# Attention's lead-in and first cycle: how bias rows are made, where the tails are turned, in which order bias rows and tails are asked for

## The chip, the core and the metric

The kernel runs on one core of one Trainium2 chip. A core has five engines that run beside one another, each through its own list of instructions in order: TensorE (PE in the profile, with PEld for its weight loads), VectorE (DVE), ScalarE (ACT), GpSimd (POOL) and SyncE (SP), which here issues nearly all transfers. An instruction that needs another engine's result, or a transfer's, waits at the head of its list, and all behind it waits too. The metric is the device time of one execution in microseconds (us).

## The reference

Three stages; the change lies in the first. q, k and v are 2 batches x 8 heads x 576 rows x 64.

```
scores = q k^T / 8
cum    = cumsum(max(s, 0))                       # per head, over the 576 rows
bias   = -(cum[i] - cum[j])
scores = where(j > i, -1e9, scores + min(bias, 0))
attn   = softmax(scores)
x      = attn v                                  # 1152 rows x 512
x      = (h cos h) w_out, with h = x w_in        # first expert layer, 512 x 2048 and back
out    = routed experts(x)                       # top 1 of 8, w1 512 x 1024, w2 1024 x 512
```

## The kernel before, in words

**Pairs and tails.** Heads are worked two at a time: 8 pairs, numbered 0 to 7, four of each batch. Of a head's 576 rows, 512 are four full tiles of 128; the last 64, the *tail*, are kept apart, for all four pairs of a batch together (tiles `qt`, `kt`, `vt`, and `wt` for their halves). A number in float32 is carried as two float16 halves (hi and lo), and q and k are turned so that the 64 columns of a head lie along the partitions; a matmul of `qT` and `kT` then has two parts, c = 0 with hi and lo, and c = 1 with hi and six more rows that carry the bias: `cum`, split into three float16 parts, for q, and the constants for k, and the other way round. These six are the *bias rows*.

**Lead-in.** `cums` (L190) sums s by a scan, turns the sums into PSUM, copies them to `cc` and writes the three parts to `bias_`, for q and k at once. `a_first` prepares pair 0 and the tails of the first batch on the engines: hi halves by ScalarE, lo halves by GpSimd, turns by TensorE (`turn_`: four turns into one PSUM bank, and one copy out of it). For all later pairs the turned halves come by a transposing transfer (`q_T`), and the bias rows by way of DRAM: `bias_` is turned to `bT` by a transfer, stored as `bt`, and read back into `qT` and `kT` (`pair_bias`, by SyncE).

**Cycles.** Then attention runs in cycles. The table `CYCLE` holds one cycle's work as pairs of a name and an offset: in cycle i the entry (name, o) runs `o_name` for pair i - o, if there is one. `tc.keep_in_program_order` keeps each engine's list in the order in which the table emits it. So the table sets the order of all engines and of SyncE's transfers. The names that matter here: S scores (the first S of a cycle starts it on TensorE), SD and S4 scores of the tail, M the mask and minimum, E the exponential, T the turn of probabilities and C its copy, NB spreading the row sums into `rsb` on GpSimd, R turning them on TensorE, KH and KL the halves of a later pair on GpSimd, LQK the loads of q and k, BK the bias rows of k, TR q's turning transfer and its bias rows, DUP the doubling of `kT` and `qT` on GpSimd, W a weight load for the next stage. Three entries serve the second batch's tails: LT loads them (`qt`, `kt`, four transfers; pair 4 stands for the batch), KTL splits them on GpSimd, TT turns them by transfers. LT has offset -4, so it runs at the end of cycle 0; KTL has -2 and runs near the start of cycle 2, ahead of NB.

**PSUM.** Banks come in four kinds of two: `s`, `pt`, `mm`, `sm`. A new use of a kind waits until one of its two banks has been read out.

Of the kernel before, what the change touches and what calls it, by code (L numbers as in the profile page):

```python
# [36 lines left out]
PB = 3  # L37
# [38 lines left out]
def kernel(ctx, tc, q, k, v, s, w_in, w_out, wg, w1, w2, out, cap, wide):  # L76
# [115 lines left out]
    def cums(pool):  # L192
# [138 lines left out]
    def a_first(ap):  # L331
# [11 lines left out]
        def dup_(w_, f, x):
            V(nc.scalar.copy, w_[:, 1, :, 0, :], halves(w_[:, 0], x)[0])

        def turn_(w_, t, c, a, f, i):
            pt = bank(*BANKS[i % 3], F16)
            m = KB if c else 128
            for j in range(4):
                tr_(pt[0:m, j * 128:(j + 1) * 128], w_[:, c, a + j, :, :].rearrange("p b d -> p (b d)")[:, 0:m], idh)  # L350
            V(f, t[0:m, c, a:a + 4, :].rearrange("p a t -> p (a t)"), pt[0:m, 0:512])
# [8 lines left out]
        for z in tail_:  # L360
            lo_(*z)
        d["qT"], d["kT"] = room(ap, "q", 2 * FULL, PB), room(ap, "k", 2 * FULL, 2)
        tl["qT"], tl["kT"] = room(ap, "qt", NP, 2), room(ap, "kt", NP, 2)
        for w_, f, x in work_:
            o = x * BW
            V(nc.vector.tensor_copy, w_[:, 1, :, 1, 0:6], bias_[:, o:o + 12 * FULL].rearrange("p (k c) -> p k c", c=6))
        for w_, f, x in tail_:
            o = x * BW
            V(nc.vector.tensor_copy, w_[:, 1, :, 1, 0:6], bias_[:, o:o + NP * NB * 6].rearrange("p (a c) -> p a c", c=NB * 6)[:, :, 12 * FULL:12 * FULL + 6])
        i = 0  # L370
        for c in range(2):
            for w_, f, x in work_:
                for a in (0, 4):
                    turn_(w_, d["qk"[x] + "T"], c, a, nc.vector.tensor_copy if c else nc.scalar.copy, i)
                    i += 1
        for z in tail_:
            dup_(*z)
        for c in range(2):
            for w_, f, x in tail_:
# [1003 lines left out]
```

## Time and profile before

| what | us |
|---|---|
| median of 3 runs | 434.71 |
| lowest and highest | 433.16, 439.06 |
| the profiled execution | 437.53 |
| its span, first to last instruction | 435.8 |
| TensorE busy | 401.6 (92%) |
| VectorE, ScalarE, GpSimd busy | 312.6, 275.6, 150.0 |

Attention's cycles start, by their first S on TensorE, at 15.46, 23.14, 33.91, 43.72, 53.28, 63.53, 73.09 and 82.66 us; the first expert layer runs to about 196 us, and the routed experts fill the rest. In the profile a busy share is an average over stages with different limits, and matmuls are pipelined, so a busy TensorE is not TensorE at its peak. The granted clock (PEclk) tells at what share of 2.4 GHz TensorE ran; 0.50 is 1.2 GHz. A row of the timeline gives the start, the duration, the engine, the line and the tiles, written first, then `<-`, then read; SPq is SyncE's queue of transfers, and its duration is that of the issue, not of the transfer.

### The profile page before, as it was taken

To read this page: it belongs to the slowest core of one execution; us is meant where nothing else is said; L and a number is where in the kernel's file an instruction comes from. 1 tells how busy PE (TensorE), PEld (TensorE's weight loads), DVE (VectorE), ACT (ScalarE), POOL (GpSimd) and SP (SyncE) were. 2 spreads that over 40 slices of the span, in tenths; PEclk is the share of its full clock that TensorE was granted. 3 is DMA by queue.
4 is the path that set the end of the run, shared out by engine and by line. 5 is a ranking of instruction groups with operands and counts; after the bars stand their busy time and mean duration, and the time that the engine had idled before them with its cause. 6 is when DMAs were issued, how large, how long until landed. Compare 5 with 4: busy or idle time off the path is not lost.

```text
span 435.8 us, 10790 instructions
## 1 busy us (share of the span) xinstructions
PE 401.6 (92%) x4008; PEld 291.5 (67%) x4008; DVE 312.6 (72%) x767; ACT 275.6 (63%) x634; POOL 150.0 (34%) x242
## 2 busy tenths in 40 slices
PE   2799999999999999989999999797999999798893
PEld 1588888886666666544444454355988999798862
DVE  7769999749998499989875665654824576667570
ACT  6679989977888577775234433525536667677560
POOL 7668888553454345445000032010011012022030
PEclk9989999999999999999999999899999999899898
DMA  7979995103389933312567476758697689888741
GB/s 164 206 169 195 165 214 142 52 2 99 97 231 304 335 121 99 96 57 90 193 186 236 111 160 225 221 127 252 206 213 159 178 277 251 312 280 278 250 133 39
DMA packets 91228, 77.61 MB, mean 178 GB/s; under 512 B 64006, under 2 KB 72198, under 8 KB 91167
## 3 DMA queue, kind: packets, MB, share of 16 engines
q1 hardware_dynamic: 87855, 71.85, 60.2%
q0 software_dynamic: 2256, 4.73, 3.2%
q8 instruction: 33, 0.54, 0.6%
q10 hardware_dynamic: 1056, 0.26, 0.3%
q14 instruction: 28, 0.23, 0.2%
HBM read 57.66 MB, written 12.36 MB: 161 GB/s over the span
## 4 chain that ended last, share of the span: by engine, by line
PE 30%; DMA 11%; DVE 7%; ACT 5%; issue 5%; SPq 2%; POOL 1%; POOLq 0%; ACTq 0%; DVEq 0%
DMA ws<-in_moe_w_dram 9%; PE ps_mm L865 6%; PE ps_sm L865 4%; PE ps_mm L1064 3%; PE ps_s L1042 2%; PE ps_pt L865 2%; PE ps_s L865 2%; PE ps_pt L1042 2%; PE ps_pt L1064 2%; PE ps_mm L1042 2%; PE ps_s L1064 2%; DVE gall L657 2%; ACT gall L656 2%; DMA xr<-row 1%; DVE ws L679 1%
## 5 line engine op out<-in xcount | busy, mean ns | idle before, releaser
L810 PEld LDWEIGHTS <-win 128*128 128x128 f16 x576 | 56.2, 98 | 37.9 <-issue 1.1
L865 PEld LDWEIGHTS <-gall 128*128 128x128 f16 x432 | 41.3, 99 | 50.5 <-issue 4.0
L865 PE MATMUL ps_mm<-wout,gall 128*128 128x512 f16 x240 | 57.9, 387 | 1.3 <-DVE n__2934 L824 1.3
L1051 POOL DMA_INDIRECT out_dram<-gall,eM x16 | 20.2, 1266 | 101.8 <-ACT gall L1050 94.1
L657 DVE SCALAR_TENSOR_TENSOR gall<-ws,gall 128x1024 f16<-128x1024 f32 x32 | 38.7, 1220 | 23.0 <-ACT gall L656 22.6
L656 ACT ACTIVATE gall<-ws 128x1024 f16<-128x1024 f32 x32 | 33.6, 1058 | 26.9 <-DMA ws<-in_moe_w_dram 26.8
L656 ACT ACTIVATE wout<-ws 128x512 f16<-128x512 f32 (+1 forms) x32 | 27.2, 860 | 27.7 <-DVE ws L679 20.3
L239 ACT ACTIVATE z<-z,st 128x256 f32<-128x256 f32 (+4 forms) x72 | 41.9, 587 | 0.8 <-DVE st L239 0.8
L239 DVE CUSTOM_DVE_ANT_0 z<-ps_s,zm 128x512 f32<-128x512 f32 (+3 forms) x72 | 34.5, 510 | 10.2 <-PE ps_s L242 9.0
L945 POOL DMA_INDIRECT disp<-row,rsli x9 | 9.2, 1020 | 93.9 <-ACT rm L926 48.6
L657 DVE SCALAR_TENSOR_TENSOR wout<-ws,wout 128x512 f16<-128x512 f32 (+1 forms) x32 | 30.3, 954 | 10.7 <-ACT wout L656 10.6
L810 PE MATMUL ps_s<-xT,win 128*128 128x384 f16 x192 | 34.1, 326 | 0.0
L810 PE MATMUL ps_pt<-xT,win 128*128 128x384 f16 x192 | 33.8, 326 | 0.0
L810 PE MATMUL ps_mm<-xT,win 128*128 128x384 f16 x192 | 33.8, 326 | 0.0
L245 PE MATMUL ps_pt<-idf,z 128*128 128x128 f32 x192 | 30.2, 282 | 1.3 <-DVE p L239 1.3
L823 ACT ACTIVATE y<-y,quarter 128x384 f32<-128x384 f32 x48 | 29.2, 609 | 0.1
L239 ACT COPY p<-ps_pt 128x512 f32<-128x512 f32 (+2 forms) x48 | 25.2, 525 | 6.0 <-PE ps_pt L245 5.7
L657 DVE SCALAR_TENSOR_TENSOR win<-ws,win 128x1024 f16<-128x1024 f32 x16 | 19.5, 1224 | 12.4 <-ACT win L656 12.1
L1042 PEld LDWEIGHTS <-gall 128*128 128x128 f16 x480 | 27.9, 97 | 0.7 <-DVE gall L657 0.6
L245 PEld LDWEIGHTS ps_pt<-idf,z 128*128 128x128 f32 x192 | 23.1, 145 | 6.3 <-issue 1.5
L1064 PEld LDWEIGHTS <-gall 128*128 128x128 f16 x384 | 23.9, 101 | 2.8 <-issue 2.8
L242 PE MATMUL ps_s<-kT,qT 128*128 128x384 f16 (+7 forms) x128 | 24.1, 307 | 1.0 <-DMA kT<-bt 0.5
(497 smaller groups left out, 897.2 us busy)
## 6 DMA issues: line engine op xcount, KB each, us to landing
ws<-in_moe_w_dram SPq DMA_DIRECT2D x64, 512.0 KB, 5.3
ws<-in_moe_w_in_dram SPq DMA_DIRECT2D x16, 512.0 KB, 5.3
ws<-in_moe_w_out_dram SPq DMA_DIRECT2D x16, 512.0 KB, 4.0
disp<-zc SPq DMA_DIRECT2D x18, 257.0 KB, 7.2
out_dram<-zc SPq DMA_DIRECT2D x9, 256.0 KB, 4.7
qf<-in_q_dram SPq DMA_DIRECT2D x16, 128.0 KB
vf<-in_v_dram SPq DMA_DIRECT2D x16, 128.0 KB, 2.9
kf<-in_k_dram SPq DMA_DIRECT2D x14, 128.0 KB, 3.5
```

The lines of the kernel that those rows point to most:

```text
L239: return pin(f(*a, **kw))
L242: return pin(nc.tensor.matmul(out_, **kw))
L245: return pin(nc.tensor.transpose(out_, in_, id_))
L656: nc.scalar.activation(hi, src, AF.Copy, scale=sc)
L657: (eng or nc.vector).scalar_tensor_tensor(lo, src, sc, hi, ALU.mult, ALU.subtract)
L810: nc.tensor.matmul(hp[:, 0:CH], lhsT=win[a][:, kk, fs], rhs=xT[:, x_, kk, xs], start=(n == 0), stop=(n == 3 * KD - 1))
L823: nc.scalar.activation(y, y, AF.Sin, scale=TWO_PI, bias=quarter)
L865: gate["pe"] = nc.tensor.matmul(xp, lhsT=G[c][:, a, f, ts], rhs=wout[w_][:, f, :], start=(f == 0 and n == 0), stop=(f == KF - 1 and n == 2))
L945: sc = nc.gpsimd.indirect_dma_start(out=disp, out_offset=bass.IndirectOffsetOnAxis(ap=sli.bitcast(U32), axis=0), in_=r, in_offset=None, bo ...
L1042: gate["pe"] = nc.tensor.matmul(hp[:, 0:ns], lhsT=a1[:, kk, a, fs], rhs=X[:, x_ * KD + kk, 0:ns], start=(n == 0), stop=(n == 3 * KD - 1))
L1051: sc = nc.gpsimd.indirect_dma_start(out=out, out_offset=bass.IndirectOffsetOnAxis(ap=M[:, b, 1:2].bitcast(U32), axis=0), in_=y, in_offset= ...
L1064: nc.tensor.matmul(yp[:, 0:ns], lhsT=a2[:, f, w_, d * 128:(d + 1) * 128], rhs=Hh[:, a, f, :], start=(n == 0), stop=(n == 3 * KE - 1))
```

## The change

Four things are changed, all in attention.

1. `cums` no longer copies the sums to `cc` in SBUF for q and k: it rearranges them once in a PSUM bank, and VectorE splits them there, for q alone. ScalarE copies k's half of `bias_` from q's.
2. In `a_first`, ScalarE instead of VectorE puts the bias columns beside the halves; the copies out of the turns are shared out in another way; and the turns of the tails are gone. They are done by a new entry, AT, in cycle 0, with the tail's scores SD of pair 0 behind them. The tails' lo halves come later on GpSimd, behind pair 1's.
3. Transfers ahead of cycle 0 stand in another order: `bT` behind q of pair 2, `bt` early, and the bias rows of pair 1 ahead of the loads that follow.
4. In `CYCLE`, BK moves to the front, and LT goes from offset -4 to -3.

```diff
 CYCLE = (
-    ("LQK", -3), ("S", 0, 2, 1), ("KL", -1, "k"), ...
+    ("BK", -1), ("LQK", -3), ("S", 0, 2, 1), ("KL", -1, "k"), ...
...
-    ..., ("C", 1, 3, 0), ("BK", -1), ("T", 1, 0), ("KL", -2, "q"),
+    ..., ("C", 1, 3, 0), ("T", 1, 0), ("KL", -2, "q"),
...
-    ("S", 0, 0, 0), ("S", 0, 0, 1), ("DA",), ...
+    ("AT", 0), ("S", 0, 0, 0), ("S", 0, 0, 1), ("DA",), ...
...
-    ..., ("M4", 0), ("E", 0, 0, 1), ("W",), ("LT", -4),
+    ..., ("M4", 0), ("E", 0, 0, 1), ("W",), ("LT", -3),
...
-        cc = pool.tile([128, 2, B * NP, 2 * FULL + 1], F32, tag="cc", name="cc", bufs=1)
+        K9 = 2 * FULL + 1
+        cf = bank("sm", 2)[:, 0:B * NP * K9]
+        cc = cf.rearrange("p (a k) -> p a k", k=K9)
...
-            part = bias_[:, 2 * i + 1:2 * i + 1 + 2 * (BW - 1)].rearrange("p (x r) -> p x r", x=2)[:, :, 0:BW - 5:6]
+            part = bias_[:, 2 * i + 1:BW:6]
             gate["cum"] = nc.vector.tensor_copy(part, cf)
...
+        A, D_ = nc.scalar.copy, nc.vector.tensor_copy
+        jobs = [(c, w_, x, a) for c in range(2) for w_, f, x in work_ for a in (0, 4)]
+        for i, ((c, w_, x, a), f) in enumerate(zip(jobs, (A, D_, D_, A, D_, D_, D_, A))):
+            turn_(w_, d["qk"[x] + "T"], c, a, f, BANKS[i % 3])
+            if i == 0:
+                side = [bias_[:, o:o + BW].rearrange("p (r c) -> p r c", c=6) for o in (0, BW)]
+                V(nc.scalar.copy, side[1][:, :, 0:5:2], side[0][:, :, 1:6:2])
+                for v_, g, y in work_:
+                    o = y * BW
+                    V(nc.scalar.copy, v_[:, 1, :, 1, 0:6], bias_[:, o:o + 12 * FULL].rearrange("p (k c) -> p k c", c=6))
...
-        for c in range(2):
-            for w_, f, x in tail_:
-                turn_(w_, tl["qk"[x] + "T"], c, 0, nc.scalar.copy, i)
-                i += 1
...
+    def tail_low():
+        for x in range(2):
+            lo_(wt[x], tails[0]["qk"[x]], x)
+
+    def o_AT(n):
+        if n:
+            return
+        tl, ap = tails[0], pools["ap"]
+        tl["qT"], tl["kT"] = room(ap, "qt", NP, 2), room(ap, "kt", NP, 2)
+        for i, (c, x) in enumerate(((0, 0), (0, 1), (1, 0), (1, 1))):
+            turn_(wt[x], tl["qk"[x] + "T"], c, 0, nc.scalar.copy if c else nc.vector.tensor_copy, BANKS[1 + i % 2])
+        scores_d(0)
...
     def o_SD(n):
+        if n:
+            scores_d(n)
```

What moves, on three engines. VectorE, from the turned sums in PSUM (`ps_sm`) to the three parts in `bias_`, the list before (-) and now (+):

```order
-L214 COPY cc<-ps_sm 128x8x8 x2
-L217 COPY cc<-ps_sm 64x16 x2
-L221 CAST bias__100<-cc 128x2x72
-L223 TENSOR_TENSOR cc<-cc,bias__100 128x144
...
+L215 COPY ps_sm<-ps_sm 128x8x8
+L218 COPY ps_sm<-ps_sm 64x8 x2
+L221 CAST bias__100<-ps_sm 128x72
+L223 TENSOR_TENSOR ps_sm<-ps_sm,bias__100 128x72
```

The cast and the subtraction alternate to the third cast in both; now each has half the elements and reads PSUM, and the four copies of bias columns that stood behind them on VectorE are ScalarE's.

ScalarE, from the tails' last preparation (`wt`) into the first cycle's exponentials (`z`), with the copies out of the tails' turns (`qtT`, `ktT`):

```order
 L239 COPY wt_108<-wt_108 128x4x64
 L239 COPY wt_109<-wt_109 128x4x64
-L239 COPY qtT<-ps_mm 128x512
-L239 COPY ktT<-ps_s 128x512
+L239 ACTIVATE z_273,sm__267<-z_273,st 128x256
+L239 ACTIVATE z_269,sm__267<-z_269,st 128x384
+L239 ACTIVATE z_273,sm__267<-z_273,st 128x256
 L239 COPY qtT<-ps_pt 70x512
 L239 COPY ktT<-ps_mm 70x512
```

All four copies stood ahead of the first exponential; now two stand behind three of the first cycle's exponentials, and the other two are VectorE's. On TensorE the sixteen turns and SD stand between T(0, 2, 1) and S(0, 0), where before SD stood ahead of S(0, 3, 1) and the turns ahead of all scores.

SyncE, from the weight load (`ws`) at the end of cycle 0 on; `qt` and `kt` are the second batch's tails, `kT<-bt` is BK:

```order
-L675 DMA ws_91<-in_moe_w_in_dram 128x4x128
+L688 DMA ws_91<-in_moe_w_in_dram 128x4x128
+L239 DMA kT<-bt 6x8x128
+L239 DMA qf<-in_q_dram 128x4x64 x2
+L239 DMA kf<-in_k_dram 128x4x64 x2
+L239 DMA_TRANSPOSE qT<-parts_105 128x8x128
+L239 DMA qT<-bt 6x8x128
+L239 DMA vf<-in_v_dram 128x4x64 x2
+L688 DMA ws_92<-in_moe_w_in_dram 128x4x128
 L239 DMA qt<-in_q_dram 64x4x64 x2
 L239 DMA kt<-in_k_dram 64x4x64 x2
+L239 DMA kT<-bt 6x8x128
```

The tail loads followed the weight load of cycle 0 and now follow that of cycle 1, behind a whole cycle's transfers. GpSimd's list around their split is the same in both: the lo half of pair 3's k, the split of `qt` and of `kt` into `wt`, and then rsb.

## Rows read from the trace of the kernel before

**Rows 1.** Busy us per stretch: span, PE, PEld, DVE, ACT, POOL (instructions); clock; DMA share, GB/s.

```profile
23.14:33.91 10.77, 10.77 (x124) 9.31 (x123) 8.26 (x29) 8.35 (x25) 7.20 (x10) 0.88 0.82 184
33.91:43.72 9.81, 9.72 (x125) 8.45 (x123) 9.34 (x32) 9.22 (x28) 8.12 (x12) 1.00 0.92 193
43.72:53.28 9.56, 9.56 (x125) 8.45 (x123) 9.32 (x32) 9.17 (x28) 8.05 (x10) 1.00 0.99 167
53.28:63.53 10.25, 9.71 (x125) 8.45 (x123) 9.33 (x32) 9.16 (x28) 8.97 (x12) 1.00 0.93 203
130.00:160.00 30.00, 30.00 (x186) 18.06 (x185) 22.60 (x45) 21.10 (x46) 11.97 (x14) 1.00 0.86 266
```

**Rows 2.** The same view, cut finer, inside the second attention cycle.

```profile
22.50:25.50 3.00, 3.00 (x15) 2.41 (x15) 1.08 (x5) 1.05 (x4) 0.83 (x1) 0.50 0.68 142
25.50:26.00 0.50, 0.50 (x5) 0.50 (x5) 0.47 (x4) 0.27 (x1) 0.00 (x0) 0.87 0.09 9
```

**Rows 3.** Timeline (start us, us, engine, line, what, [idle before]): the bias sums.

```profile
5.78 0.35 DVE L214 COPY cc<-ps_sm 128x64 f32<-128x64 f32 x2 [0.42 <-PE ps_sm L209]
...
6.28 1.15 POOL L239 TENSOR_TENSOR first<-qf,first 128x512 f16<-128x512 f32 x1 [2.33 <-ACT first L239]
...
6.53 1.18 DVE L221 CAST bias__100<-cc 128x144 f16<-128x144 f32 x1
...
10.27 0.71 DVE L221 CAST bias__100<-cc 128x144 f16<-128x144 f32 x1
```

**Rows 4.** Timeline of turns, copies and first scores in the first cycle.

```profile
12.13 0.61 PE L245 MATMUL ps_pt<-idh,first 128*70 128x128 f16 x4 [2.44 <-DVE first L239]
...
12.77 0.42 DVE L239 COPY qT<-ps_pt 70x512 f16<-70x512 f16 x1
...
15.46 0.94 PE L242 MATMUL ps_s<-kT,qT 128*128 128x384 f16 x6
...
15.91 0.60 ACT L239 COPY ktT<-ps_mm 70x512 f16<-70x512 f16 x1
...
19.06 0.39 PE L242 MATMUL ps_s<-kT,qT 128*128 128x128 f16 x4
...
22.26 1.08 PE L245 MATMUL ps_pt<-idf,z 128*128 128x128 f32 x4 [1.27 <-DVE p L239]
```

**Rows 5.** Timeline of SyncE's queue: issues of transfers.

```profile
23.52 2.30 SPq L239 DMA_DIRECT2D vf<-in_v_dram  x2
...
26.47 1.27 SPq L239 DMA_DIRECT2D qt<-in_q_dram  x2
27.84 1.25 SPq L239 DMA_DIRECT2D kt<-in_k_dram  x2
...
34.77 1.12 SPq L675 DMA_DIRECT2D ws<-in_moe_w_in_dram  x1
35.95 1.07 SPq L239 DMA_DIRECT2D qf<-in_q_dram  x2
```

**Rows 6.** Tile kt, 27.8 to 29.1 us: from issue to landing.

```profile
DMA to landing us min/median/max: 3.4/3.4/3.4
```

**Rows 7.** Timeline of GpSimd: the second batch's tails and the row sums.

```profile
32.94 0.40 POOL L239 CAST wt<-qt 128x256 f16<-128x256 f32 x1
...
34.03 0.40 POOL L239 CAST wt<-kt 128x256 f16<-128x256 f32 x1
...
34.51 0.67 POOL L239 TENSOR_TENSOR wt<-kt,wt 128x256 f16<-128x256 f32 x1
...
36.49 0.61 POOL L239 COPY rsb<-rs 128x512 f32<-128x512 f32 x1 [1.31 <-PE ps_s L242]
```

**Rows 8.** Timeline of TensorE: the turn of rsb, and a wait for kT.

```profile
37.69 0.60 PE L245 MATMUL ps_mm<-idf,rsb 128*128 128x128 f32 x4
...
54.14 0.77 PE L242 MATMUL ps_s<-kT,qT 70*128 70x384 f16 x5 [0.54 <-DMA kT<-bt]
```

**Rows 9.** DMA queues, 23.5 to 26 us: packets, MB, share of 16 engines.

```profile
q8 instruction: 1, 0.02, 3.4%
```

More of the change, by code (lines that the diff above doesn't have):

```diff
@@ L357, in a_first @@
             dup_(*z)
+        d["qT"], d["kT"] = room(ap, "q", 2 * FULL, PB), room(ap, "k", 2 * FULL, 2)
+        A, D_ = nc.scalar.copy, nc.vector.tensor_copy
[8 more added lines that the diff above has]
+                    V(nc.scalar.copy, v_[:, 1, :, 1, 0:6], bias_[:, o:o + 12 * FULL].rearrange("p (k c) -> p k c", c=6))
@@ L358, in a_first @@
         for z in tail_:
             hi_(*z)
[L360 to L366, printed above, removed]
         for w_, f, x in tail_:
             o = x * BW
-            V(nc.vector.tensor_copy, w_[:, 1, :, 1, 0:6], bias_[:, o:o + NP * NB * 6].rearrange("p (a c) -> p a c", c=NB * 6)[:, :, 12 * FULL:12 * FULL + 6])
@@ L370, in a_first, with turn_ @@
-        i = 0
-        for c in range(2):
-            for w_, f, x in work_:
-                for a in (0, 4):
-                    turn_(w_, d["qk"[x] + "T"], c, a, nc.vector.tensor_copy if c else nc.scalar.copy, i)
-                    i += 1
+            V(nc.scalar.copy, w_[:, 1, :, 1, 0:6], bias_[:, o:o + NP * NB * 6].rearrange("p (a c) -> p a c", c=NB * 6)[:, :, 12 * FULL:12 * FULL + 6])
         for z in tail_:
             dup_(*z)
-        for c in range(2):
-            for w_, f, x in tail_:
-                turn_(w_, tl["qk"[x] + "T"], c, 0, nc.scalar.copy, i)
-                i += 1
+    def turn_(w_, t, c, a, f, b_):
+        pt = bank(*b_, F16)
+        m = KB if c else 128
+        for j in range(4):
+            tr_(pt[0:m, j * 128:(j + 1) * 128], w_[:, c, a + j, :, :].rearrange("p b d -> p (b d)")[:, 0:m], idh)
+        V(f, t[0:m, c, a:a + 4, :].rearrange("p a t -> p (a t)"), pt[0:m, 0:512])
@@ new lines, in lo_ @@
+    def lo_(w_, f, x):
+        hi, lo = halves(w_[:, 0], x)
+        V(nc.gpsimd.tensor_tensor, lo, f, hi, ALU.subtract)
+    def tail_low():
[9 more added lines that the diff above has]
+        scores_d(0)
@@ L623, in attention @@
         wl = win_jobs(NW0)
-        load_qk(ap, 2)
+        bT = ap.tile([128, NBT, 128], F16, name="bT")
+        load(ap, 2, "q", q, 2)
+        V(nc.sync.dma_start_transpose, out=bT, in_=bias_)
+        load(ap, 2, "k", k, 2)
         for x in range(2):
             cast_pair(1, x)
-        bT = ap.tile([128, NBT, 128], F16, name="bT")
+        tail_low()
+        V(nc.sync.dma_start, bt[0:NBT * 128, :].rearrange("(b p) t -> p b t", p=128), bT)
         load(ap, 0, "v", v, 3)
-        V(nc.sync.dma_start_transpose, out=bT, in_=bias_)
         q_T(ap, 1)
-        load_tail(ap, 0, "v", v, 2)
-        wl["load"]()
-        V(nc.sync.dma_start, bt[0:NBT * 128, :].rearrange("(b p) t -> p b t", p=128), bT)
-        load_qk(ap, 3)
         k_room(ap, 1)
@@ L637, in attention @@
             pair_bias(1, x)
+        load_tail(ap, 0, "v", v, 2)
+        wl["load"]()
+        load_qk(ap, 3)
         V(nc.sync.dma_start, wg_sb, wg.rearrange("(k p) e -> p k e", p=128))
-        ops_ = {f.__name__[2:]: f for f in (o_S, o_M, o_E, o_T, o_C, o_SD, o_S4, o_M4, o_M4b, o_E4, o_T4, o_T4b, o_C4, o_C4b, o_N, o_NB, o_V, o_R, o_X, o_RC1, o_RC2, o_XS1, o_XS2, o_XT, o_PX, o_KH, o_KL, o_LQK, o_LV, o_TR, o_BK, o_KT, o_CK, o_DUP, o_LT, o_KTL, o_TT, o_DT)}
+        ops_ = {f.__name__[2:]: f for f in (o_S, o_AT, o_M, o_E, o_T, o_C, o_SD, o_S4, o_M4, o_M4b, o_E4, o_T4, o_T4b, o_C4, o_C4b, o_N, o_NB, o_V, o_R, o_X, o_RC1, o_RC2, o_XS1, o_XS2, o_XT, o_PX, o_KH, o_KL, o_LQK, o_LV, o_TR, o_BK, o_KT, o_CK, o_DUP, o_LT, o_KTL, o_TT, o_DT)}
         last = max(c[1] for c in CYCLE if len(c) > 1 and c[0] != "D")
```

18 lines of the change are left out of this document (4 added, 14 removed), and 8 rows, old and new, of the table CYCLE.

## The prediction

> **What bounds the kernel now.** I read the busy time of each engine first, cut at the start of each attention cycle, because the change lies in the first 60 us. From the second cycle on TensorE has no gap: it is busy 10.77 of 10.77 us in the cycle that starts at 23.14 and 9.56 of 9.56 us in the one that starts at 43.72, and between 130 and 160 us, in the first expert layer, it is again busy all the time [rows 1]. So an attention cycle costs TensorE 9.56 us when nothing is late, and what is over that is a loss with a cause. Two cycles show one. The cycle from 23.14 takes 1.21 us more, and its granted clock is 0.88; the finer cut shows why: the clock stands at 0.50, which is 1.2 GHz, from 22.5 to 25.5 us, and is back at 2.4 GHz for most of the half microsecond after that [rows 2]. It had fallen after TensorE stood still for 1.27 us before the turn at 22.26 [rows 4]. The cycle from 53.28 takes 0.69 us more at a full clock [rows 1]; TensorE waits 0.54 us there for kT<-bt, k's bias rows [rows 8].
>
> Then I read the queues. SyncE issues nearly every transfer, one behind another, and the reader is to see that it never rests: the tail loads of the second batch are issued from 26.47 to 29.09 us, the weight load of the next cycle from 34.77 us, and the row behind it starts at 35.95 us [rows 5]. GpSimd splits those tails into halves when it reaches them at 32.94 us, ends at 35.18 us, and spreads the row sums (rsb) from 36.49 us, with 1.31 us to spare [rows 7]. TensorE turns rsb (R) at 37.69 us [rows 8]. Nothing there waits for the tails, because they were asked for 6.5 us before GpSimd came to them.
>
> **The change, part by part.** (a) *The bias sums.* Before, VectorE takes from 5.78 to 10.98 us: two copies, two small ones, three casts and two subtractions. A cast that starts at 6.53 us, just behind a GpSimd subtraction of 1.15 us that started at 6.28 us, takes 1.18 us and ends 0.28 us behind it, and the last still takes 0.71 us for 144 elements; the copy of 64 elements out of PSUM, started when GpSimd was idle, takes 0.18 us [rows 3]. After, there are eight instructions, half as wide, that read PSUM. Bounds: 0.18 us each (ends at 7.2 us) or the old mean of 0.58 us (5.2 / 9; ends at 10.4 us). I take the short one, since the casts' lengths follow GpSimd and the PSUM copy has half their elements at a quarter of the time. ScalarE's extra copies (216 elements, and two of 48) lie between 0.2 and 0.6 us each, the latter being its copy of 512 [rows 4]; I take 0.4, 0.3 and 0.3 us. They stand behind the first turn's copy, so the bias columns are in place at about 9.5 us and the turns that need them follow the others without a break. With four such groups of turns, 0.61 us each at most, and the last copy of 0.60 us, the first scores come at about 11.9 us instead of 15.46 us [rows 4]: 3.6 us earlier, 1.5 if the casts stay slow.
>
> The Trainium skill, page "SBUF — State Buffer", section "Who interferes with whom", says that a VectorE instruction with at most one SBUF input outside its two-port modes does not contend with GpSimd, while copies, casts and two-SBUF-input forms do. By it (a) ends at the short bound; no row of before shows these very instructions.
>
> (b) *The tails' turns within the cycle.* The 16 turns leave the lead-in and stand in front of SD and S(0,0) now, and two ScalarE copies stand in the middle of its exponentials. TensorE cannot take S(0,0) before SD, SD needs both ScalarE copies, and the third group of turns needs VectorE's copy of the first. S(0,0) started 3.60 us after the first scores (19.06 - 15.46) [rows 4]. Now four groups at up to 0.61 us, one VectorE copy of 0.42 us and two ScalarE copies of 0.60 us stand there [rows 4]: 4.1 us, of which some 1.5 us run beside what was there. So about 2.6 us of the 3.6 are given back, and the second cycle starts some 1 us earlier than 23.14 us (0 to 2). (c) *k's bias rows first* (BK): the request passes the four q and k loads, 1.07 us for a pair of them [rows 5]. The 0.54 us wait at 54.14 us goes, with 0.15 us of TensorE start-up: -0.69 us [rows 1, 8]; it stays only if the second half of attention runs further ahead than now.
>
> (d) *The tail loads move one cycle later (LT -4 to -3).* This is the term that decides. The four loads now stand behind the second cycle's weight load, while GpSimd's split of them stands where it stood, ahead of rsb. SyncE's list ahead of the loads is otherwise the list before: 35.95 less the loads' own 2.67 us (26.47 to the end at 29.09, and a gap) is 33.28 us [rows 5]. The new waits early in the list (for the finished bias, for its turned copy, for its arrival in DRAM) against the old ones I put at +0.4 us (-0.8 to +1.8, the upper end being bt's whole landing as now). So the loads start at 33.7 us; k's second half is issued 2.0 us later (27.84 + 1.25 / 2 - 26.47) and lands 3.4 us behind its issue [rows 5, 6]: 39.1 us. The split of k takes 1.15 us from then (34.03 to 35.18), rsb 0.61 us [rows 7]: 40.85 us. TensorE's R then starts at about 40.8 instead of 37.69 us: **+3.1 us** (+1.9 to +4.5). Behind R on TensorE stand the rest of the cycle's turns, scores and value products, and ScalarE and VectorE live from them; behind GpSimd's split stand rsb, the copy of the attended rows, the next q halves and the doubling of kT and qT, all as late but with as much room as before. The microsecond won in (b) is lost in this wait, since the loads are bound by the queue and not by TensorE.
>
> (e) *The clock.* TensorE would be at R by 36.4 us (37.69 less 1 and 0.25) and stands still for over 4 us. It fell to half after 1.27 us of rest before, and stayed there for 3.4 us: the cycle in which that lay lost 1.21 us, and the 0.43 us by which the four turns at 22.26 us (1.08 us) exceed a group at full clock (0.61 us, close to it) come on top [rows 1, 2, 4]. So **+1.7 us** (0 if the clock holds).
>
> Sum: 3.1 + 1.7 - 0.7 = **+4.1 us**. From 64 us on TensorE is the bound until past 160 us, and the weight loads behind that are released by buffers that the kernel itself frees, so the shift goes through to the end. The profiled execution took 437.53 us (span 435.8 us), which is 2.8 us over the median of 434.71 us; a shift is a shift, so 438.8 us against the median, 441.6 us in a profile like that one.
>
> SyncE's stall in the value load at 23.52 us (two issues in 2.30 us, against 1.07 us for two q loads of the same size) has a packet of 0.02 MB on an instruction queue in its stretch [rows 5, 9]. The Trainium skill, page "Runtime: NRT & Kernel Launch", section "Instruction fetch mechanics", says that such a refill is mostly hidden behind the engine's own issue. By that the stall is a chance one that need not come back: the loads would start 1.3 us earlier and the sum would be +2.8 us. The row contradicts it, and I keep the stall, since the same number of rows stands ahead.
>
> **The rivals.** *The queue is in time (faster).* If SyncE runs through its list without its stalls, the tail loads start near 30 us and k's tail lands by 35 us; then GpSimd ends rsb by 36.8 us and TensorE meets no wait worth the name. Then the first cycle's 1 us stays, and both kT waits go (0.25 us in the cycle from 33.91, the excess over 9.56, and 0.69): -2.0 us, 432.7 us; -3.7 if the clock keeps up too. For it: issues of 0.5 us each, as in the q loads, would be enough. Against: the list ahead of the loads ran almost without rest before, and the point at which it decides, k's tail landed by 35.4 us, is 2.5 us ahead of my lowest bound. *The clock holds.* GpSimd's wait comes, but TensorE returns at 2.4 GHz: +2.4 us, 437.1 us. For it: the exact moment of a fall follows no row. *The loss is absorbed.* A later wait, such as that for expert weights, hides it: 434.7 us. Against: those loads wait for buffers that are late as well. *It gets deeper.* The late transfers meet the next cycle's and the wait repeats: +7 us, 441.7 us.
>
> **How the numbers follow.** The forecast has 0.50, the held clock 0.20, the queue in time 0.17, absorbed 0.08, deeper 0.05. The range from 433.0 to 441.5 us takes in the forecast's own (436.3 to 441.2: 1.9 + 1.7 - 0.7 to 4.5 + 1.7 - 0.7, with less on the low side if the clock holds), the held clock, the absorbed loss and half of the queue in time: 0.83 or a little more. A change of 2%, about what a measurement of this kernel can tell from none, is 8.7 us here. No case reaches that; I leave 0.02 for faster and 0.04 for slower, 0.94 for the rest.
>
> **What would show it.** In the profile after: bias casts near 0.2 us and first scores near 12 us (a); S(0,0) more than 5 us behind the first scores (b); no wait for kT<-bt (c); the qt loads issued near 33.7 us, GpSimd's cast of the tails near 37 to 39 us instead of 32.94 us, R near 40.8 us behind a wait for rsb (d); half clock in the microseconds after that (e). Wrong would be (d) above all: if GpSimd casts the tails before 35 us, the change gains its 2 us.

## The result, and the profile after

The changed kernel takes 440.60 us (median of 20 runs, 438.01 to 444.15), the kernel before in runs taken with it 435.37 us (431.55 to 439.06): a ratio of 1.0117 with a 95% interval from 1.0091 to 1.0143, some 5.1 us slower. The forecast was 438.8 us, with a range from 433.0 to 441.5 us. The profiled execution took 444.15 us, with a span of 442.2 us. Ratios compare undisturbed runs alone; one kernel below (e5) had too few of them for a ratio, and the profile of another (e3) is of a disturbed run, read here for attention only.

I cut TensorE's time again at the starts of the cycles, now 10.99, 21.83, 33.35, 50.34 and 59.90 us. The columns are the stretch, its length, TensorE's busy time with its instructions, the granted clock, the DMA share and GB/s.

```profile
10.99:21.83 10.84, 7.66 (x58) 0.87 0.84 191
21.83:33.35 11.52, 11.52 (x124) 0.83 1.11 182
33.35:50.34 16.99, 11.60 (x125) 0.80 0.57 131
50.34:59.90 9.56, 9.56 (x125) 1.00 0.87 184
```

The first cycle starts 4.47 us earlier than before (10.99 against 15.46) [rows 4], the second only 1.31 us earlier, and the third takes 16.99 us where it took 9.81 [rows 1]. From 50 us on each cycle costs its 9.56 us. The whole loss lies between 21 and 50 us.

The starts of S lie close to places where TensorE is late or early by accident, so from here on I read time by R, the turn of the row sums, of which every cycle has one. "Last R" is that of the last pair, the end of attention for our purpose.

| | before | after | difference |
|---|---|---|---|
| R, first | 27.88 | 27.32 | -0.56 |
| first to second R | 9.81 | 15.11 | +5.30 |
| second to third R | 9.56 | 11.44 | +1.88 |
| third to fourth R | 10.25 | 9.56 | -0.69 |
| last R | 93.98 | 99.92 | +5.94 |

The first four differences sum to +5.93 us, which is the shift of the last R and, within the noise, that of the medians. Where the 5.30 us come from is read in the three queues. First SyncE's, as in [rows 5]:

```profile
23.61 2.40 SPq L239 DMA_DIRECT2D vf<-in_v_dram  x2
...
28.18 2.30 SPq L239 DMA_DIRECT2D kf<-in_k_dram  x2
...
33.73 1.34 SPq L688 DMA_DIRECT2D ws<-in_moe_w_in_dram  x1
35.17 1.27 SPq L239 DMA_DIRECT2D qt<-in_q_dram  x2
36.55 1.25 SPq L239 DMA_DIRECT2D kt<-in_k_dram  x2
```

The tail loads are issued at 35.17 us, where they were issued at 26.47. GpSimd, the answer to [rows 7]:

```profile
39.59 0.40 POOL L239 CAST wt<-qt 128x256 f16<-128x256 f32 x1 [7.22 <-DMA qt<-in_q_dram]
...
40.68 0.40 POOL L239 CAST wt<-kt 128x256 f16<-128x256 f32 x1
...
41.77 0.61 POOL L239 COPY rsb<-rs 128x512 f32<-128x512 f32 x1
```

It stands still for 7.22 us until qt is there, splits the tails, and only then spreads rsb, 5.28 us later than before. TensorE, the answer to [rows 8]:

```profile
42.43 1.12 PE L245 MATMUL ps_mm<-idf,rsb 128*128 128x128 f32 x4 [5.39 <-POOL rsb L239]
```

R waits 5.39 us for rsb, and its four turns take 1.12 us in place of 0.60: the clock is at half. The view cut by single microseconds shows how long, behind R and, above it, in the first two cycles (to be set beside [rows 2]):

```profile
19.00:20.00 1.00, 0.69 (x5) 0.52 0.75 203
...
22.00:25.00 3.00, 3.00 (x15) 0.50 1.55 119
25.00:26.00 1.00, 1.00 (x6) 0.57 0.65 141
...
43.00:44.00 1.00, 1.00 (x6) 0.50 0.00 0
...
46.00:47.00 1.00, 1.00 (x16) 0.83 1.04 202
```

Half clock lasts from R to a little past 46 us, 3.9 us. Of the two stretches the earlier one is new in its length: 6.8 us, from 19.0 to some 25.9 us, where before it was about 3.4 us, from 22.2 to 25.6.

### The profile page after: what moved, and what is told of

The parts are those of the page before. It is cut to its first block, busy times and chain, and to the rows that moved or that the text cites. A ratio compares the mean times of both kernels' runs of the same rounds, so it can differ in the third digit from the quotient of the medians.

```text
span 442.2 us, 10786 instructions
## 1 busy us (share of the span) xinstructions
PE 403.7 (91%) x4008; PEld 293.1 (66%) x4008; DVE 309.6 (70%) x765; ACT 275.6 (62%) x636; POOL 150.4 (34%) x242
## 4 chain that ended last, share of the span: by engine, by line
PE 62%; DMA 14%; DVE 8%; ACT 6%; issue 5%; SPq 2%; POOL 2%; POOLq 0%; ACTq 0%; DVEq 0%
DMA ws<-in_moe_w_dram 12%; PE ps_mm L878 6%; PE ps_s L823 6%; PE ps_mm L823 6%; PE ps_pt L823 6%; PE ps_pt L245 5%; PE ps_s L242 5%; PE ps_sm L878 4%; PE ps_mm L242 4%; PE ps_pt L878 2%; PE ps_s L878 2%; DVE gall L670 2%; ACT gall L669 2%; PE ps_s L1055 2%; PE ps_mm L1077 2%
## 5 line engine op out<-in xcount | busy, mean ns | idle before, releaser
L878 PEld LDWEIGHTS <-gall 128*128 128x128 f16 x432 | 41.3, 98 | 49.8 <-issue 3.1
L245 PE MATMUL ps_pt<-idf,z 128*128 128x128 f32 x192 | 31.7, 292 | 0.9 <-DVE p L239 0.6
L1055 PEld LDWEIGHTS <-gall 128*128 128x128 f16 x480 | 27.9, 97 | 0.7 <-DVE gall L670 0.7
L245 PEld LDWEIGHTS ps_pt<-idf,z 128*128 128x128 f32 x192 | 24.1, 150 | 6.5 <-ACT z L239 1.0
L242 PE MATMUL ps_s<-kT,qT 128*128 128x384 f16 (+7 forms) x128 | 25.3, 320 | 0.8 <-DVE st L239 0.4
L669 ACT ACTIVATE win<-ws 128x1024 f16<-128x1024 f32 x16 | 16.9, 1056 | 14.3 <-DMA ws<-in_moe_w_dram 14.3
```

Of the source, the lines that this page charges most:

```text
L242: return pin(nc.tensor.matmul(out_, **kw))
L245: return pin(nc.tensor.transpose(out_, in_, id_))
L669: nc.scalar.activation(hi, src, AF.Copy, scale=sc)
L878: gate["pe"] = nc.tensor.matmul(xp, lhsT=G[c][:, a, f, ts], rhs=wout[w_][:, f, :], start=(f == 0 and n == 0), stop=(f == KF - 1 and n == 2))
L1055: gate["pe"] = nc.tensor.matmul(hp[:, 0:ns], lhsT=a1[:, kk, a, fs], rhs=X[:, x_ * KD + kk, 0:ns], start=(n == 0), stop=(n == 3 * KD - 1))
```

## The experiments

Two theories were tried by kernels that differ from one of the two in a place or two: that the late tail loads make the loss, through the split that waits ahead of rsb and the clock behind it; and, as its rival, that the new order of the bias rows and the tails' turns within the first cycle do. The table holds the R of each profiled execution and the ratio to the kernel before with its 95% interval; what each kernel is follows below.

| kernel | R first, second, third | last R | ratio |
|---|---|---|---|
| before | 27.88, 37.69, 47.25 | 93.98 | 1 |
| after | 27.32, 42.43, 53.87 | 99.92 | 1.0117 [1.0091, 1.0143] |
| e1 | 27.03, 36.59, 46.15 | 92.78 | 0.9971 [0.9941, 1.0002] |
| e2 | 26.94, 42.02, 53.05 | 99.10 | 1.0141 [1.0093, 1.0188] |
| e3 | 27.36, 36.92, 47.56 | 93.89 | 0.9949 [0.9913, 0.9985] |
| e4 | 26.00, 42.88, 54.09 | 100.14 | 1.0057 [1.0024, 1.0091] |
| e5 (after, again) | 27.44, 42.57, 54.05 | 100.10 | none |
| e6 | 27.79, 43.83, 53.38 | 99.43 | 1.0047 [1.0009, 1.0085] |
| e7 | 27.52, 37.86, 47.42 | 93.47 | 0.9960 [0.9927, 0.9993] |
| e8 | 26.43, 35.99, 45.88 | 93.19 | 0.9949 [0.9907, 0.9991] |
| e9 | 28.43, 37.99, 47.55 | 93.60 | 0.9943 [0.9886, 1.0001] |
| e10 | 28.00, 40.02, 51.24 | 97.29 | 1.0088 [1.0029, 1.0148] |
| e11 | 28.27, 37.83, 47.39 | 93.44 | 0.9996 [0.9940, 1.0052] |

### e1 and e2: the late tail loads, undone and alone

e1 is the changed kernel with this one edit:

```
-("W",), ("LT", -3),
+("W",), ("LT", -4),
```

> The changed kernel with the tail loads of the next batch put back where they stood (LT -4); all else is as changed. Theory (the late tail loads cost the wait and the clock; the rest of the change gains): in the second cycle GpSimd no longer waits for qt, TensorE's R comes at about 36.4 us (the 42.43 us of the changed kernel less 5.39 us of wait and what the half clock costs ahead of it), no later turn at half clock, every cycle 9.56 us from R to R, and the end of attention 1.3 + 0.7 us earlier than in the kernel before: ratio 0.995 (0.992 to 0.998), some 8 us faster than the changed kernel. Rival (the tails' turns within the first cycle and the new order of the bias cost the time): about as slow as the changed kernel, ratio 1.010.

The ratio is 0.9971 (0.9941 to 1.0002): the loss is gone, and the expected 0.995 lies inside the interval, as does no gain at all. GpSimd's and TensorE's timelines:

```profile
32.02 0.40 POOL L239 CAST wt<-qt 128x256 f16<-128x256 f32 x1
...
35.40 0.61 POOL L239 COPY rsb<-rs 128x512 f32<-128x512 f32 x1 [1.14 <-PE ps_s L242]
...
36.59 0.60 PE L245 MATMUL ps_mm<-idf,rsb 128*128 128x128 f32 x4
...
52.93 0.77 PE L242 MATMUL ps_s<-kT,qT 70*128 70x384 f16 x5 [0.41 <-DMA kT<-bt]
```

There is no wait for qt, R comes at 36.59 us at full clock, and the next one 9.56 us later. But from the third R to the fourth it is 10.13 us: the last row shows that a wait for k's bias rows is left, 0.41 us where it was 0.54 [rows 8]. So that part of the expectation was wrong: moving BK first did not by itself end this wait.

e2 is the kernel before with the opposite edit, LT -4 to -3, and nothing else.

> The kernel before with one edit: the tail loads one cycle later (LT -3). Theory: the loads are issued behind the weight load near 33.3 us, GpSimd waits for qt until about 38 us, R comes near 40.5 to 41 us instead of 37.69 us with TensorE at rest for 3 us or more, half clock behind it, the wait for k's bias rows stays or is hidden behind the new wait: ratio 1.010 to 1.014 (+4.5 to +6 us). Rival (the queue's stalls come from the new order of the bias rows and value loads): the loads are in time or nearly, +0 to +2 us, ratio 1.000 to 1.004.

The ratio is 1.0141 (1.0093 to 1.0188). This one entry of the table makes the whole loss without any other part of the change. Its SyncE, GpSimd and TensorE:

```profile
27.53 1.71 SPq L239 DMA_DIRECT2D kf<-in_k_dram  x2
...
33.37 1.26 SPq L675 DMA_DIRECT2D ws<-in_moe_w_in_dram  x1
34.68 1.28 SPq L239 DMA_DIRECT2D qt<-in_q_dram  x2
...
39.19 0.40 POOL L239 CAST wt<-qt 128x256 f16<-128x256 f32 x1 [7.07 <-DMA qt<-in_q_dram]
...
42.02 1.12 PE L245 MATMUL ps_mm<-idf,rsb 128*128 128x128 f32 x4 [5.35 <-POOL rsb L239]
```

The tail loads are issued at 34.68 us, 1.4 us later than the sum of the prediction had for this very case without the other parts (33.28 us). In the first trace of the changed kernel it is 0.49 us more, but six profiles of kernels with that list up to the loads (after, e3, e4, e5, e6, e8) have it anywhere from 33.75 to 35.26 us, so this difference says nothing by itself.

### e3: the same late loads, with the split behind what TensorE needs

```
-("KL", -1, "k"), ("KTL", -2), ("RC2", 2),
+("KL", -1, "k"), ("RC2", 2),
 ...
-("T", 1, 0), ("KL", -2, "q"),
+("T", 1, 0), ("KL", -2, "q"), ("KTL", -2),
```

> The changed kernel with the tail loads as late as there (LT -3), but GpSimd's split of the tails (KTL) moved in its list from ahead of rsb to behind the next q halves, so that nothing that TensorE turns stands behind that wait in the same cycle. Theory (it is the place of the waiting split ahead of rsb that costs, not the load's lateness itself): qt is still issued near 35 us and lands near 39.5 us, but rsb is spread at about 36 us, R comes near 36.5 us, no fall of the clock: ratio 0.993 to 0.998, as the kernel with the early loads. Rival (the late loads hold up something else too: the copies of the tails, the turns TT, the queue behind them): R in time, but a wait of 2 us or more some us later, ratio 1.003 to 1.010.

GpSimd's and TensorE's timelines:

```profile
35.72 0.61 POOL L239 COPY rsb<-rs 128x512 f32<-128x512 f32 x1 [3.32 <-PE ps_s L242]
...
36.92 0.60 PE L245 MATMUL ps_mm<-idf,rsb 128*128 128x128 f32 x4
...
39.46 0.40 POOL L239 CAST wt<-qt 128x256 f16<-128x256 f32 x1 [0.72 <-ACT z L239]
...
43.83 0.78 PE L242 MATMUL ps_s<-kT,qT 70*128 70x384 f16 x5 [0.55 <-POOL qT L239]
```

The loads are issued at 35.06 us, as late as in the changed kernel, and the split starts at 39.46 us, as late as there. But rsb no longer stands behind it: R comes at 36.92 us, and the ratio is 0.9949 (0.9913 to 0.9985). So the lateness by itself makes little of the loss; most of it is made by what stands behind the late thing in an engine's list. The new place has a price too, which begins with the last row: the doubling of qT now stands behind the split, and TensorE waits 0.55 us for it, and 0.18 us for GpSimd's `parts` in the cycle after. From the second R to the fourth it takes 20.48 us in place of 19.12, twice 9.56: 1.36 us.

### e10: the queue's dose

The changed kernel with two neighbours of the table exchanged, so that the tails pass the weight load:

```
-("W",), ("LT", -3),
+("LT", -3), ("W",),
```

> The changed kernel with the two last steps of a cycle exchanged: the late tail loads are issued ahead of the weight load (W) of the same cycle and no longer behind it. Theory (R moves with the moment at which SyncE reaches the tail loads, one for one): qt issued 1.3 to 1.5 us earlier, near 33.7 us, GpSimd's split 38.1 us, R near 41.0 us in place of 42.4, 4 us of rest, half clock behind it as before (some 11.4 us to the next R): ratio 1.005 to 1.009. Rival (the transfers themselves are slow there, as other traffic holds the DMA queues until 39 us): split and R move by less than 0.5 us, ratio 1.009 to 1.014.

SyncE's, GpSimd's and TensorE's timelines:

```profile
33.21 1.29 SPq L239 DMA_DIRECT2D qt<-in_q_dram  x2
...
37.09 0.40 POOL L239 CAST wt<-qt 128x256 f16<-128x256 f32 x1 [4.03 <-ACT p L239]
...
40.02 0.66 PE L245 MATMUL ps_mm<-idf,rsb 128*128 128x128 f32 x4 [2.30 <-POOL rsb L239]
```

qt is issued 1.96 us earlier than in the changed kernel, and R comes 2.41 us earlier, so the rival, that they move by less than 0.5 us, is out. But the theory, one for one with the issue, is not shown either. In a second trace of the changed kernel (e5, below) qt was asked for at 33.75 us, only 0.54 us later than here, and GpSimd began its split at 39.73 us, 2.64 us later than here. What e10 changes besides the moment is that the weight load no longer stands ahead of the tails; whether that transfer ahead of them holds them up, no run shows apart. The time is 0.3% less than the changed kernel's by the ratios (1.0088 against 1.0117), with intervals that overlap; the last R is 2.63 us earlier. Behind R the clock falls again, after a rest of 2.30 us only, as the cut by microseconds shows:

```profile
40.00:41.00 1.00, 0.98 (x7) 0.80 1.25 277
41.00:42.00 1.00, 1.00 (x5) 0.50 1.36 219
...
43.00:44.00 1.00, 1.00 (x10) 0.50 0.36 74
44.00:45.00 1.00, 1.00 (x18) 1.00 1.02 193
```

From this R to the next it takes 11.22 us: a wait less than half as long brought the same loss by the clock, less 0.2 us.

### e4 and e6: keeping TensorE busy during the wait

Both are the changed kernel with matmuls added ahead of R of the second cycle, N = 18 in e4 and 30 in e6; R overwrites what they write.

```
+if n == 1:
+    for _ in range(N):
+        mm_(rp, lhsT=idh, rhs=first[0][:, 0, 0:4].rearrange("p a b d -> p (a b d)"), start=True, stop=True)
```

> The changed kernel with 18 matmuls more (128 x 512, in the second cycle only, ahead of R and into R's bank, where R overwrites them), so that TensorE works through most of its wait for rsb; the wait itself stays. Theory (the fall of the clock behind the wait costs 1.7 to 1.9 us): R at 42.4 us as in the changed kernel, its turns at full clock (0.60 us for four instead of 1.12 us), the cycle behind it 9.56 to 9.8 us from R to R instead of 11.44 us, ratio to the kernel before 1.007 to 1.009, 1.7 us faster than the changed kernel. Rival (the half clock costs nothing, since other engines bound that cycle): R to R stays above 11 us, ratio 1.012. If the 18 matmuls run at half clock they take over 7 us and delay R; then R's start says so.

TensorE's timeline in e4:

```profile
35.56 4.05 PE L242 MATMUL ps_mm<-first,idh 128*128 128x512 f16 x18
42.88 0.66 PE L245 MATMUL ps_mm<-idf,rsb 128*128 128x128 f32 x4 [3.27 <-POOL rsb L239]
...
46.24 1.07 PE L242 MATMUL ps_s<-kT,qtT 128*64 128x512 f16 x4
```

The 18 matmuls ended before rsb came, TensorE still rested for 3.27 us, and R's turns ran at nearly full clock, but it then fell: the scores at 46.24 us take 1.07 us in place of 0.60. From R to R it took 11.21 us. That did not tell the theories apart, so e6 covers the wait to its end.

> As e4, but with 30 matmuls ahead of R of the second cycle in place of 18. In e4 the 18 took 4.05 us, TensorE rested for 3.27 us behind them, and the clock fell all the same, a little over a microsecond after R. 30 take some 6.7 us and end near 42.3 us, just ahead of rsb. Theory (the clock falls because TensorE rests): no half clock behind R, 9.6 us from R to R in place of 11.2 to 11.4, 1.7 us faster than the changed kernel: ratio 1.006 to 1.008. Rival (something else than the clock holds that cycle, or other work falls behind): R to R stays near 11.2 us, ratio 1.011.

TensorE's timeline in e6:

```profile
37.35 6.64 PE L242 MATMUL ps_mm<-first,idh 128*128 128x512 f16 x30
43.83 0.60 PE L245 MATMUL ps_mm<-idf,rsb 128*128 128x128 f32 x4
```

Now the clock holds, and from R to R it takes 9.55 us in place of 11.44. So the half clock behind R costs 1.89 us, and it comes from the rest. R itself is late by what the added matmuls overran: rsb was there at 42.24 us (GpSimd's copy of 0.61 us from 41.63), R started at 43.83. The sum of both fits the last R, 99.43 us against 99.92. The ratios of e4 and e6 (1.0057 and 1.0047) are lower than that of the changed kernel by more than their last R says (100.14 and 99.43): 2.6 and 3.0 us against -0.2 and +0.5. Behind attention, and ahead of the last microseconds, these profiles have one to three more stretches of half clock, in places that change (near 280, 374 and 405 us in that of before, at 304 us alone in e2's); the mean granted clock of the whole execution, over all runs of a kernel, was 0.976 in the changed kernel (twenty runs), 0.981 in e4 and 0.987 in e6 (twelve each). So the two ran less at half clock elsewhere too; why, stays open.

### e5: the changed kernel again

> The changed kernel itself, timed on the same chip as the next three. Both theories: ratio 1.009 to 1.014, the wait for qt on GpSimd 6.5 to 9 us, R at 42 to 43 us and 11.2 to 11.5 us from that R to the next.

On TensorE the trace repeats the first to 0.2 us: R at 27.44, 42.57 and 54.05 us behind a wait of 7.24 us for qt on GpSimd, last R at 100.10 us. Six runs took 435.81 to 445.26 us. SyncE's list does not repeat the first trace:

```profile
33.75 1.97 SPq L239 DMA_DIRECT2D qt<-in_q_dram  x2
...
39.73 0.40 POOL L239 CAST wt<-qt 128x256 f16<-128x256 f32 x1 [7.24 <-DMA qt<-in_q_dram]
```

qt is asked for 1.42 us earlier than in the first trace and is there no earlier: from its issue to its landing the profile gives 5.2 us, where the first has 3.6. So an earlier issue alone did not bring R forward.

### e7: the tails' turns back in the lead-in

e1 with the second part of the change undone: the four groups of turns stand at the end of `a_first` again, and GpSimd's halves of the first tails (`tail_low`) ahead of the second pair's.

```
-("AT", 0), ("S", 0, 0, 0),
+("S", 0, 0, 0),
 ...
 def a_first(ap):
     ...
+    tail_low()
     ...
+    for i, (c, x) in enumerate(((0, 0), (0, 1), (1, 0), (1, 1))):
+        turn_(wt[x], tl["qk"[x] + "T"], c, 0, nc.scalar.copy if c else nc.vector.tensor_copy, BANKS[(2 + i) % 3])
```

> The kernel of e1 (early tail loads, new bias sums, k's bias rows first) with the 16 turns of the first tails back in the lead-in, ahead of the first scores, and SD of the first cycle back at its place behind them; GpSimd's halves of those tails stand ahead of the second pair's again. It undoes the second part of the change alone. Theory (turning them in the cycle is worth a little): ScalarE's six small copies and four groups of turns stand ahead of the first scores, which come near 15 us instead of 10.84; S(0,0) comes 3.6 us behind them, near 18.6 us instead of 18.2; the second cycle starts 0.3 to 1 us later than the 21.67 us of e1: ratio 0.998 to 1.000. Rival (the turns in the cycle cost what the lead-in gains): second cycle no later than in e1, ratio 0.997 or less.

TensorE's timeline in e7:

```profile
13.10 0.40 PE L245 MATMUL ps_mm<-idh,wt 128*128 128x128 f16 x4 [1.74 <-POOL wt L239]
...
14.41 2.15 PE L242 MATMUL ps_s<-kT,qT 128*128 128x384 f16 x8
```

The first scores come at 14.41 us in place of 10.84 in e1, behind a wait for GpSimd's halves. These wait for ScalarE's hi halves of the tails, which come at 11.88 us, where they came at 7.65 in the kernel before: e7 brings back the old place of the turns, not the whole old lead-in. At the first R the 3.57 us have shrunk to 0.49 (27.52 against 27.03), and the ratio of 0.9960 (0.9927 to 0.9993) can't be told from e1's 0.9971. Turning the tails within the cycle is worth half a microsecond in these two executions, and nothing that the times can tell. (Behind that R, e7 also waits 0.62 us for kT<-bt, at 34.50 us, which e1 does not.)

### e9 and e11: the wait for k's bias rows

e9 is the kernel before with BK moved to the front of the table, and nothing else.

> The kernel before with one edit: the request for k's bias rows (BK) first in each cycle, ahead of the q and k loads. Theory (the request is 1.1 to 1.7 us earlier in SyncE's list, and the wait of 0.54 us with it gone): every cycle from the third on 9.56 us from R to R, no wait for kT<-bt, attention ends 0.7 us earlier: ratio 0.996 to 1.000. Rival (what stands ahead of it in the list, the transposes of the tails, decides, as in e1, where a wait of 0.41 us was left): the wait shrinks to 0.1 to 0.4 us, ratio 0.998 to 1.001.

In SyncE's timeline k's bias rows for the fifth cycle are asked for ahead of the q and k loads now:

```profile
48.52 0.35 SPq L239 DMA_DIRECT2D kT<-bt  x1
```

That request started at 50.50 us before. TensorE has no wait at all from 24 to 100 us, every cycle takes 9.56 us (the last two less, as before), and from the first R to the last it takes 65.17 us in place of 66.10: 0.93 us less, the 0.69 us and the 0.25 us by which the cycle from 33.91 exceeded 9.56 [rows 1]. The ratio is 0.9943 (0.9886 to 1.0001), too wide to show 0.9 us by itself.

In e1 the same edit had left 0.41 us, with the request at 48.77 us. e11 is e1 with the second batch's tail turns (TT), four requests that stand ahead of this one and take 3.64 us of issues in e1's trace, one cycle later:

```
-("TR", -2), ("TT", -2),
+("TR", -2),
 ...
-("BK", -1), ("LQK", -3),
+("BK", -1), ("LQK", -3), ("TT", -1),
```

> The kernel of e1 (tail loads early, GpSimd's split where it was) with the turns of the second batch's tails by transfer (TT) one cycle later, behind the q and k loads of the fourth cycle. In e1 a wait of 0.41 us for kT<-bt is left in the fifth cycle, with these four requests (5.7 us of SyncE) ahead of k's bias rows. Theory (SyncE's order alone decides that wait): no wait for kT<-bt, 9.56 us from R to R throughout, attention ends at 92.2 us or a little after, ratio 0.992 to 0.997. Rival (the requests now hold up the next transposes or rows instead): a wait of 0.4 us or more for qT or kT one cycle later, ratio 0.995 to 0.999.

Now the request for k's bias rows comes 4.85 us earlier than in e1:

```profile
43.92 0.34 SPq L239 DMA_DIRECT2D kT<-bt  x1
```

No wait is left from 24 to 100 us, and each cycle takes 9.56 us. From the first R to the last it is 65.17 us, as in e9; the last R comes at 93.44 us and not at 92.2, since the first one came at 28.27 us, 1.24 us later than in e1. A TensorE that is 1.24 us later would have covered e1's wait of 0.41 us by itself, so e11 alone does not show that SyncE's order decides. The ratio of 0.9996 (0.9940 to 1.0052) says nothing on so small a step.

### e8: late loads, with room for everything

The changed kernel with KTL moved behind the doubling of kT and qT, and TT one cycle later:

```
-("KL", -1, "k"), ("KTL", -2), ("RC2", 2),
+("KL", -1, "k"), ("RC2", 2),
 ...
-("DUP", -1, 0), ("DT", -1),
+("DUP", -1, 0), ("KTL", -2), ("DT", -1),
 ...
-("BK", -1), ("LQK", -3),
+("BK", -1), ("LQK", -3), ("TT", -1),
 ...
-("TR", -2), ("TT", -2),
+("TR", -2),
```

> The changed kernel, its tail loads as late (LT -3), with GpSimd's split of them moved behind the doubling of kT and qT, in the same cycle, and their turns by transfer (TT) one cycle later, first in SyncE's list behind the q and k loads. In e3 the split behind the next q halves held up qT for 0.55 us. Theory (only work that TensorE needs soon must not stand behind the split): no wait on TensorE of over 0.3 us between 24 and 62 us, 9.56 us from R to R, attention ends some 2 us earlier than in the kernel before (-1.3 from the lead-in, -0.7 from its wait for kT): ratio 0.993 to 0.996. Rival (the queue gets late elsewhere, at TR's transposes or k's bias rows, since TT stands ahead of them now): a wait of 0.5 us or more for qT or kT in the fourth or fifth cycle, ratio 0.996 to 1.000.

GpSimd's and TensorE's timelines:

```profile
51.71 0.61 POOL L239 COPY qtT<-qtT 64x512 f16<-64x512 f16 x1 [1.41 <-DMA qtT<-wt]
...
56.09 0.62 PE L245 MATMUL ps_sm<-idh,parts 128*128 128x128 f16 x8 [1.00 <-POOL parts L239]
```

No wait for qT or kT is left, but one of 1.00 us for `parts`, k's halves from GpSimd. It does not come from the split: GpSimd waits 1.41 us for the tails' turning transfer (TT), one cycle later now, and the k halves stand behind the doubling of these tails. So the theory missed a second reader that waits, and the rival had the cause, TT's place, but not the tile. For the wait on k's bias rows e8 is the better test: with TT out of the way its third R came at 45.88 us, earlier than e1's 46.15, and there was none. The last R comes at 93.19 us, and the ratio is 0.9949 (0.9907 to 0.9991). With e3 (0.9949) and e7 (0.9960) it is one of three versions whose intervals lie under 1: some 2 us faster than the kernel before, 7 us faster than the changed one. Among themselves they can't be told apart.

## Why the prediction was right, and where it was off

**The mechanism was right, (d) and (e).** Late tail loads, a split that waits ahead of rsb, a late R, half clock behind it: each step stands in the profile after; e2 makes the loss with LT alone, e1 takes it away with LT alone, and e3 shows that the place ahead of rsb is what costs.

**The size of (d) was too small:** R at 42.43 us in place of 40.8, +4.74 us against +3.1 (the range's +4.5 was just passed). The term that was mis-sized is the arrival of the tails. The working had both split by 40.2 us (39.1 + 1.15); they were split by 41.77 us in the first trace and by 41.91 in the second. In the first the loads are issued late, at 35.17 us instead of 33.7, and landing takes about what I had (3.6 us against 3.4); from there on the working holds (35.17 + 2.0 + 3.4 + 1.15 + 0.61 gives 42.33 us for the end of rsb). Part of that lateness is that I moved all that follows the loads' old place forward by their 2.67 us. In e2 the weight load moved by 1.40 (33.37 against 34.77 us): two kf issues took 1.71 us there, k's bias rows 0.87 and the weight load 1.26, where they had taken 1.00, 0.29 and 1.12; why is not shown. But in the second trace (e5) the loads were issued at 33.75 us, where I had them, and R came at 42.57 all the same, since the landing took 5.2 us and not 3.4. So an issue in time would not have made the sum right, and what keeps qt from landing before 39 us in both traces stays open. Nor can the +0.4 us for the new bias waits be read from these traces, whose issue varies by 1.5 us. That GpSimd begins at q's landing, and splits both tails behind it, 2.18 us in sum, I had worked out as k's split behind k's landing; in the first trace it comes to the same.

**(e) was right:** 1.88 us against 1.7, and e6, without the rest, shows 1.89 us less. (In its sum the turns at 22.26 us exceed a full-clock group by 0.47 us, 1.08 less 0.61, and not by 0.43.) "The clock holds" was ruled out three times over: after rests of 5.39, 3.27 and 2.30 us it fell.

**(c) was right in size,** -0.69 us, and e9 shows the edit alone doing it, with the 0.25 us of another cycle. But in e1 it did not. There the rows were asked for at 48.77 us, hardly later than in e9 (48.52), and TensorE was 1.40 us further ahead (second R at 36.59 against 37.99 us): the exception that the prediction had named. With TT's requests moved away as well the wait was gone, in e8 even with TensorE earlier than in e1; e11 alone does not show it. In the changed kernel the late R gave the rows time as well, so its trace alone could not have shown whose merit it was.

**(a) was right in direction, and somewhat larger:** first scores at 10.99 us against 11.9, and those of the second part at 11.86 us, behind ScalarE's copy. VectorE's timeline, the answer to [rows 3]:

```profile
5.79 0.23 DVE L215 COPY ps_sm<-ps_sm 128x64 f32<-128x64 f32 x1 [0.41 <-PE ps_sm L209]
...
6.55 0.40 DVE L221 CAST bias__100<-ps_sm 128x72 f16<-128x72 f32 x1
...
8.00 0.40 DVE L221 CAST bias__100<-ps_sm 128x72 f16<-128x72 f32 x1
```

The sums end at 8.4 us, not at 7.2 as eight instructions of 0.18 us would, nor at 10.4. GpSimd's two subtractions run from 6.13 to 8.40 us beside them, and no cast is stretched to the end of one, as the one of 1.18 us was [rows 3]. That agrees with the rule of the Trainium skill, page "SBUF — State Buffer", section "Who interferes with whom", that a VectorE instruction with at most one SBUF input, outside the two-port modes, does not contend with GpSimd (copies and casts, it says, can contend). Since the casts have half their elements now as well, the trace does not separate the two. And a cast of 72 elements takes 0.40 us all the same, so 0.18 us from the copy was too short a row for it.

**(b) was too small.** 4.47 us were won by the first scores, and 3.6 us of them given back by S(0,0) (18.21 against 19.06 us) in place of the 2.6 forecast; at the second cycle 1.31 us were left, close to the 1 of the forecast, but at the first R only 0.56. TensorE's timeline shows the two places:

```profile
16.61 0.38 PE L245 MATMUL ps_pt<-idh,wt 128*70 128x128 f16 x4 [0.68 <-DVE qtT L239]
...
18.15 0.22 PE L242 MATMUL ps_sm<-ktT,qtT 70*128 70x128 f16 x1 [0.87 <-ACT ktT L239]
...
20.93 1.11 PE L245 MATMUL ps_pt<-idf,z 128*128 128x128 f32 x4 [0.56 <-DVE p L239]
```

Turned within the cycle, the tails make TensorE wait for two copies, 0.68 and 0.87 us, where in the lead-in nothing was behind. The clock falls at 19 us here and not at 22.2, and the second cycle runs its first 4 us at 1.2 GHz, where before it was 2.5. The other traces say much the same: with the turns within the cycle the half clock of the first two cycles lasted 6.8 us in seven profiles and 3.4 in two (e4, e8); with the lead-in of before it lasted 3.4 us in two (before, e9) and was absent in e2. The prediction had the waits in its sum, but no cost of the clock in these cycles. That the two waits lengthen the half clock is likely but not shown; e7, without them, had 6.8 us of it as well, from 14.6 us. How much time it costs in an average run can't be said from single profiles: kernels with the same lead-in as e1 had their first R between 26.00 and 28.27 us, those with the lead-in of before at 26.94 (without any half clock), 27.88 and 28.43.

**The stall of SyncE** in the value load was no chance: 2.40 us in the changed kernel, 2.25 in e2, 2.15 in e1; in e9 the two value loads took 0.94 us, and the weight load behind them 1.53 us in place of 0.51. By the rule of the Trainium skill, page "Runtime: NRT & Kernel Launch", section "Instruction fetch mechanics", a fetch would have been mostly hidden, and the loads 1.3 us earlier. Some such stall came back in every trace; if it is the fetch, they don't agree with that rule for SyncE, but none shows that the fetch is its cause.

In sum: +3.1 + 1.7 - 0.7 was forecast and +4.74 + 1.88 - 0.69 came out; of the difference of 1.8 us, 1.6 is R's lateness and 0.2 the clock. The medians moved by 5.2 us. That the result lies in the range is partly luck: the forecast's own terms add up to 437.6 to 440.2 us (434.71 with 2.9 to 5.5 us) and not, as written, to 436.3 to 441.2, and 440.60 us is just above them. The shift of the medians, 5.2 us, is inside.

## What to carry to other kernels

When a load is moved later in a queue, look up what stands behind its first reader on that reader's engine: e3 kept the loads as late and moved the reader, and from the first R to the last it took 66.53 us, where the changed kernel took 72.60 and e1, with early loads, 65.75. Work taken out of a queue that looks full need not bring the rest forward by its whole length; in e2 it was 1.40 of 2.67 us. Nor does an earlier issue mean an earlier landing: in two traces of one kernel the issues of qt lie 1.42 us apart, and GpSimd had it within 0.14 us of the same time. And a wait on TensorE is paid twice: once by its length, and once by what runs at half clock behind it, 1.9 us here for a wait of 5.4 us and still 1.7 for one of 2.3.

## What was not expected of the hardware

- A rest of 2.30 us was enough for the clock to fall (e10), but not at once: TensorE was back at work for about half a microsecond at full clock, and only then stood at 0.50 for some 3 us. After 5.39 us it was at half when TensorE came back; after 3.27 us (e4) it fell over a microsecond behind R.
- With the same instructions up to there, the kernel before had half clock from 22.2 to 25.6 us and e2 had none at all; its first R came 0.94 us earlier. Executions of the same instructions differ by that much.
- 30 matmuls that compute nothing of use, in the place of a rest, gave back the whole 1.9 us of the clock.
